# Dense layers in token order with expert results added onto them, and queries laid out like keys, in a fused attention and mixture-of-experts kernel

## The chip, the cores and the metric

The kernel runs on one core of a Trainium2 chip. The metric is the device time of one execution in microseconds (us). The five engines that matter are TensorE (PE, with its weight loads PEld), VectorE (DVE), ScalarE (ACT), GpSimd (POOL) and SyncE (SP). SP computes nothing: it issues most of the transfers, in the order of its own queue. POOL issues the indirect transfers (scatters) and the weight loads.

## The reference

Eight heads of sliding-window attention over 8 batches of 576 tokens are followed by a mixture of experts. Every token gets a dense two-layer result, and the result of the one expert with the largest gate logit, scaled by its probability:

```python
scores = scale * q @ k.T + bias; mask = (rel >= 0) & (rel < 128)
attn_out = softmax(where(mask, scores, -1e9)) @ v          # 8 x 8 x 576 x 64
x = attn_out.transpose(0, 2, 1, 3).reshape(4608, 512)
y_dense = relu(x @ w1_dense) @ w2_dense                     # 512 -> 512 -> 512
e = argmax(x @ w_gate); gate = softmax(x @ w_gate)[e]       # 8 experts
out = y_dense + gate * (relu(x @ w1[e]) @ w2[e])            # 4608 x 512, float32
```

## The kernel before

**Attention** runs in 16 units (`u`): a unit is one batch and four of its eight heads. A unit loads keys, queries and values (`load_k`, `load_q`, `load_v`, all on SP), turns keys and queries on DVE (`turn`, lines 310 and 313), rounds them on ACT (lines 319 and 323), makes scores on PE into the PSUM tiles `sq0` and `sq1` (lines 517 and 534), takes their exponentials on ACT (line 545, tile `p`), splits off a low part on DVE (line 555), multiplies with the values on PE (line 586, tile `ax`) and divides on DVE (`norm`, lines 604 to 616). `norm` of a batch's second unit ends with its last 64 rows, line 616. PE then transposes the result (line 646), and ACT copies it out of PSUM (line 655). Of the loads, `load_k` is one transfer with 4,608 bytes in a row; `load_q` is four transfers (one for each head) with 512 bytes in a row, because the queries come in another interleaving than the keys. The mask pattern and the list of token numbers (`place_f`) follow this interleaving.

**Routing**, once a batch: logits on PE, the choice of the expert and the position within it on DVE, and five scatters on POOL (`send`, line 809), which put the batch's rows of bfloat16, with gate and token number, into `xs_dram`, sorted by expert.

**Blocks.** A block is 128 rows of one expert, and there are 43 of them. Twenty are early: 11 may run after batch 4, another 9 after batch 6. The other 23 are late: they wait for all rows of the last batch. For a block, SP fetches the rows with a transposing transfer into `xTm` (line 958) and gate and token number into `xm` (line 961). DVE copies the expert's first weights (`bring`, line 997). PE runs `layer1` (line 1007) twice, once with the expert's weights and once with the dense ones; ACT applies relu twice; PE runs `layer2` (line 1019) twice; ACT scales the expert's result by the gate (line 1030); DVE adds the dense result (`sum_y`, line 1033); and POOL scatters the sum to the rows of the output (`store`, line 1037). So the dense layers run on the sorted rows too, 43 x 128 = 5,504 of them with the padding.

**Buffers** come from rings (`ROOMS`): `xm` has four places, which `store` still reads, early blocks have one `ye` and one `yo`, `stg` (turned keys and queries) has two. In the late blocks `p` (six places) holds weights and results.

**The order** on each engine is fixed before the run: a planner walks over the parts of the work, with costs, dependencies and wished times (`PACE`, `PLACE`, one offset and one step for each kind of part), and writes down an order for each engine. Engines and queues keep to it: an instruction that waits holds up all that stands behind it on its engine.

## Time and profile before

| | |
|---|---|
| runs of the kernel before | 420.17, 417.85, 414.70 us; median 417.85 |
| the profiled execution | 416.41 us, of which its trace spans 414.6 |
| mean granted clock of PE | 0.936 of full speed |
| busy: PE, DVE, POOL, ACT | 322.8, 269.4, 226.0, 203.3 us |
| DMA | 59.62 MB, mean 144 GB/s |

Busy time is the time in which an engine has an instruction under way. Matmuls are pipelined, so PE can count as busy while the next matmul is not yet needed. "Idle before" is an engine's pause in front of an instruction, with what ended it. The span divides into attention alone (to about 175 us), attention with early blocks (to about 283), routing of the last batch with the remaining early blocks (to about 319), and late blocks.

### The profile page before, as it was taken

The page shows a single profiled execution, that of the slowest core. Times are in us where ns is not written, and L with a number is a line of the kernel's source. Part 1 is how long each engine was busy: PE and PEld are TensorE (multiplying, and loading weights), DVE is VectorE, ACT ScalarE, POOL GpSimd, SP SyncE. Part 2 cuts the span into 40 slices and gives each one's busy share as a digit, 9 for nine tenths or more (in the row PEclk, how much of TensorE's full clock was granted, in tenths as well). Part 3 has the DMA queues.
Part 4 walks back from the last instruction along what each step waited for, and adds up shares of the span by engine and source line. Part 5 has one row for each costly group of instructions (what it writes and reads, how often), then busy time and mean ns, then how long its engine had stood idle before and what let it go on. Part 6 is the DMA issues. An engine that isn't in the chain of part 4 may idle for free.

```text
span 414.6 us, 12784 instructions
## 1 busy us (share of the span) xinstructions
PE 322.8 (78%) x5147; PEld 246.5 (59%) x5147; DVE 269.4 (65%) x454; ACT 203.3 (49%) x298; POOL 226.0 (55%) x269
## 2 busy tenths in 40 slices
PE   3326685876766766889798998997778879999993
PEld 0215574665665654777576776775556557767671
DVE  3268789799598898896778988755524322334331
ACT  4443564555544635474485675443243433544442
POOL 6065135996864858982668568485452422333332
PEclk9999689797769889699899999999999999999998
DMA  9994989889999967599897662125563332334430
GB/s 177 209 225 72 223 172 192 174 199 240 185 187 186 225 121 181 120 161 203 200 204 158 179 144 72 42 93 87 129 170 76 107 85 56 93 87 128 70 116 0
DMA packets 105961, 59.62 MB, mean 144 GB/s; under 512 B 71727, under 2 KB 100399, under 8 KB 105904
## 3 DMA queue, kind: packets, MB, share of 16 engines
q1 hardware_dynamic: 89952, 34.55, 42.3%
q0 software_dynamic: 14736, 23.68, 26.4%
q10 hardware_dynamic: 1216, 0.59, 0.8%
q8 instruction: 41, 0.67, 0.7%
q14 instruction: 16, 0.13, 0.1%
HBM read 47.29 MB, written 17.13 MB: 155 GB/s over the span
## 4 chain that ended last, share of the span: by engine, by line
PE 26%; DVE 25%; issue 21%; POOL 12%; DMA 10%; ACT 3%; SPq 2%; POOLq 1%; DVEq 0%; ACTq 0%
DVE p L555 11%; PE ax L586 10%; POOL out_dram L1037 8%; DMA out_dram<-yo,xm 5%; PE sq L534 4%; PE misc L1007 4%; DVE xf L605 3%; PE misc L1019 3%; DVE stg L310 3%; PE misc L646 3%; DMA vf<-in_v_dram 2%; DVE stg L313 2%; POOL xs_dram L809 2%; ACT p L545 1%; DMA rawq<-in_q_dram 1%
## 5 line engine op out<-in xcount | busy, mean ns | idle before, releaser
L555 DVE TENSOR_TENSOR p<-p 128x1024 bf16<-128x1024 f32 x64 | 101.2, 1609 | 10.6 <-ACT p L545 9.0
L586 PE MATMUL ax<-vf,p 128*128 128x65 bf16 (+3 forms) x1728 | 80.1, 208 | 11.1 <-DVE p L555 9.7
L586 PEld LDWEIGHTS <-p 128*128 128x128 bf16 (+1 forms) x1728 | 73.6, 110 | 19.7 <-DVE p L555 10.3
L545 ACT ACTIVATE p<-sq 128x1024 f32<-128x1024 f32 x64 | 63.2, 1022 | 31.9 <-PE sq L534 31.3
L809 POOL DMA_INDIRECT xs_dram<-xrow,slot x40 | 47.4, 1186 | 32.0 <-POOL xrow L806 9.3
L1037 POOL DMA_INDIRECT out_dram<-p,xm x23 | 24.7, 1076 | 55.0 <-DVE p L1033 55.0
L627 POOL CAST xrow<-xf 128x512 bf16<-128x512 f32 x32 | 35.7, 1117 | 32.8 <-DVE xf L605 32.7
L331 POOL TENSOR_TENSOR vf<-vf 128x1280 bf16<-128x1280 f32 x15 | 38.8, 2592 | 22.5 <-DMA vf<-in_v_dram 21.6
L1019 PE MATMUL misc<-w_all,hT 128*128 (+1 forms) x160 | 41.3, 384 | 7.8 <-DVE yo L1033 5.2
L1037 POOL DMA_INDIRECT out_dram<-yo,xm x20 | 24.7, 1236 | 33.3 <-DVE yo L1033 25.0
L1007 PEld LDWEIGHTS <-w_all 128*128 128x128 bf16 x688 | 40.2, 98 | 4.1 <-issue 2.9
L646 PE MATMUL misc<-ident_f,xf 128*128 128x128 f32 x128 | 24.3, 320 | 21.4 <-DVE xf L605 15.1
L1346 ACT ACTIVATE hT<-misc 128x512 bf16<-128x512 f32 x40 | 23.9, 598 | 34.3 <-PE misc L1007 34.2
L534 PE MATMUL sq<-qT,kT 32*128 32x256 f32 (+2 forms) x640 | 29.5, 314 | 10.9 <-ACT qT L319 10.0
L1277 ACT ACTIVATE xT<-sq 128x512 bf16<-128x512 f32 x46 | 25.0, 594 | 25.9 <-PE sq L1007 22.8
L655 ACT COPY xT<-misc 128x512 f32<-128x512 f32 x32 | 18.8, 587 | 34.0 <-PE misc L646 34.0
L534 PEld LDWEIGHTS sq<-qT,kT 32*128 32x128 f32 (+1 forms) x640 | 23.6, 206 | 18.5 <-ACT qT L319 11.4
L313 DVE STREAM_TRANSPOSE stg<-rawk 128x576 f32<-128x576 f32 x32 | 23.0, 759 | 14.2 <-DMA rawk<-in_k_dram 14.2
L1019 PEld LDWEIGHTS <-xT 128*128 128x128 bf16 x184 | 17.5, 98 | 23.9 <-ACT xT L1277 3.4
L646 PEld LDWEIGHTS misc<-ident_f,xf 128*128 128x128 f32 x128 | 15.9, 160 | 26.0 <-DVE xf L605 13.8
L1033 DVE TENSOR_TENSOR yo<-misc,ye 128x512 f32<-128x512 f32 x20 | 13.8, 688 | 23.7 <-DMA out_dram<-yo,xm 20.8
L517 PE MATMUL sq<-mask,ident 32*32 32x512 bf16 x512 | 20.4, 418 | 9.1 <-ACT p L545 7.2
(126 smaller groups left out, 531.7 us busy)
## 6 DMA issues: line engine op xcount, KB each, us to landing
rawk<-in_k_dram SPq DMA_DIRECT2D x16, 576.0 KB, 5.3
rawq<-in_q_dram SPq DMA_DIRECT2D x60, 144.0 KB, 5.3
vf<-in_v_dram SPq DMA_DIRECT2D x64, 128.0 KB, 4.8
w_all<-in_moe_w_dram POOLq DMA_DIRECT2D x16, 512.0 KB, 7.5
xs_dram<-fill_x SPq DMA_DIRECT2D x8, 130.0 KB, 2.0
w_all<-in_moe_w_dense_dram POOLq DMA_DIRECT2D x2, 512.0 KB
vf<-in_v_dram SPq DMA_DIRECT2D x16, 64.0 KB, 5.7
xTm<-xs_dram SPq DMA_TRANSPOSE x43, 4.1
```

Of the source, the lines that this page charges most:

```text
L313: nc.vector.transpose(out=s[:, c].rearrange("p (r x e) -> p r e x", r=R // 2, e=2), in_=raw[:, :, c].rearrange("p (r e) x -> p r e x", e=2),)
L331: eng.tensor_tensor(out=vb[:, :, :, 0:D, 0], in0=vf[:, :, :, 0:D], in1=vb[:, :, :, 0:D, 1], op=ALU.subtract,)
L534: nc.tensor.matmul(out=sq[g // 2][:nk, g % 2, PCOL[kj] : PCOL[kj] + nq], lhsT=kT[r0 : r0 + n, c, kj * P : kj * P + nk], rhs=qT[r0 : r0 + n ...
L545: nc.scalar.activation(out=p32, in_=T[(f"sq{p}", u, r)], func=ACT.Exp, scale=SCALE)
L555: nc.vector.tensor_tensor(out=lo, in0=T[("p", u, r, p)], in1=hi, op=ALU.subtract)
L586: nc.tensor.matmul(out=ax[:rows, i, o0 : o0 + w], lhsT=lhs, rhs=rhs, start=(n == 1), stop=(n == 3 * len(kl)),)
L627: nc.gpsimd.tensor_copy(out=xrows[b % 2].bitcast(BF16)[:, 2 * r : 2 * r + 2, hq * 256 : hq * 256 + 256], in_=T[("xf", u)][:, 2 * r : 2 * r ...
L646: nc.tensor.transpose(out=tp[:, i, c, :], in_=T[("xf", u)][:, 2 * r + i, c * P : c * P + P], identity=ident_f,)
L809: ins = nc.gpsimd.indirect_dma_start(out=xs_dram[:, :], out_offset=bass.IndirectOffsetOnAxis(ap=gst["slot", b][:rows, t : t + 1], axis=0), ...
L1007: nc.tensor.matmul(out=hp[:, c * P : c * P + P], lhsT=ws[:, kc, c * P : (c + 1) * P], rhs=xT[:, kc, :], start=(kc == 0), stop=(kc == 3),)
L1019: nc.tensor.matmul(out=y, lhsT=hT[:, c * P : c * P + P], rhs=w_all[:, E, 1, c, :] if dense else w_all[:, bass.DynSlice(er, 1), 1, c, :], s ...
L1037: ins = nc.gpsimd.indirect_dma_start(out=out[:, :], out_offset=bass.IndirectOffsetOnAxis(ap=T["xm", j][1].bitcast(I32)[:, 1:2], axis=0), i ...
```

## The change

The dense layers leave the blocks. Once a batch's attention is done, they run over its 576 rows in token order (`dense1`, `dense_relu`, `dense2`, `dense_out`), on a bfloat16 copy of the transposed result that ACT makes (`keep_b`, `keep_tail_b`), in the PSUM tiles `sq0`, `sq1` and `misc`; and SP stores them to the output (`dense_store`, three transfers a batch). A block then has the expert's layers alone, and its scatter adds onto the output in the transfer (`compute_op=ALU.add`). It waits for the dense stores of the batches that it can hold. `sum_y` is gone. Of the late blocks every second one (`ROWS`) is fetched as plain rows, into the space of the value buffers, and transposed on PE (`flip_rows`) with one more copy on ACT. Queries are loaded, turned and rounded as keys are: one transfer instead of four, two transposes on DVE instead of one. Rings change: `stg` 2 to 1, `hT` 3 to 2, `ye` 1 to 2, no `yo`, new `mt` (gate and token number, ten places) and `xr` (twelve). `PACE` and all of `PLACE` are new numbers.

```diff
-PACE = [11.15, 18.09]
+PACE = [10.39, 11.86]
...
-    "tt": (-36.78, 8.14), "vl": (-10.27, 9.4), "w": (24.71, 6.6), "xx": (2.02, 12.91),
+    "dy": (34.21, 3.45), "eb0": (-22.31, 9.54), "eb1": (31.4, 6.64), "ebt": (11.77, 12.23),
...
-        "stg": 2,
+        "stg": 1,
...
+        "mt": 10,
+        "xr": 12,
-        "hT": 3,
-        "ye": 1,
-        "yo": 1,
+        "hT": 2,
+        "ye": 2,
+        "xTb": 1,
+        "hTd": 1,
...
-    def load_q(u, h, eng):
...
-            out=t[32 * h : 32 * h + 32].rearrange("p (g r) c d -> p g (r c d)", r=2),
-            in_=q[b, 4 * hq + h].rearrange("(g p r) d -> p g (r d)", p=32, r=2),
+    def load_qk(u, nm, eng):
...
+            in_={"q": q, "k": k}[nm][b, 4 * hq : 4 * hq + 4].rearrange(
+                "h (p r) d -> (h p) (r d)", r=R
...
-        if nm == "q":
-            nc.vector.transpose(out=s.rearrange("p c (r x) -> p r c x", r=R), in_=raw)
-            return
         for c in range(2):
             nc.vector.transpose(
...
+    def keep_b(u, r):
...
+        nc.scalar.copy(
+            out=T[("xTb", b)][
+                :, 2 * hq : 2 * hq + 2, 2 * P * r : 2 * P * r + 2 * P
+            ].rearrange("p c (t x) -> p t c x", t=2),
+            in_=T[("misc", "tp", u, r)],
+        )
...
+    HS = S // 2
+
+    def dense1(b, c):
+        hp = buf((f"sq{c % 2}", "d", b, c), [P, 2, BANK], F32)
+        for i in range(2):
+            for kc in range(4):
+                nc.tensor.matmul(
+                    out=hp[:, i, 0:HS],
+                    lhsT=w_all[:, E, 0, kc, c * P : (c + 1) * P],
+                    rhs=T[("xTb", b)][:, kc, i * HS : (i + 1) * HS],
...
+    def dense_relu(b, c):
...
+        nc.scalar.activation(
+            out=T[("hTd", b)][:, c, :].rearrange("p (i x) -> p i x", i=2),
+            in_=T[(f"sq{c % 2}", "d", b, c)][:, :, 0:HS],
+            func=ACT.Relu,
...
+    def dense2(b, i):
+        tok = (f"sq{i}", "e", b, i) if i < 2 else ("misc", "e", b)
...
+        for t in range(2 if i < 2 else 1):
+            r0 = (2 * i + t) * P
+            rows = min(P, S - r0)
+            for c in range(4):
+                nc.tensor.matmul(
+                    out=y[:, t, :] if i < 2 else y[:rows, :],
+                    lhsT=T[("hTd", b)][:, c, r0 : r0 + rows],
+                    rhs=w_all[:, E, 1, c, :],
...
+    def dense_out(b, i):
+        t = buf(("p", "e", b, i), [P, 2, BANK], F32)
+        if i < 2:
+            nc.scalar.copy(out=t, in_=T["dy", b, i])
...
+    def dense_store(b, i):
...
+            ins = nc.sync.dma_start(
+                out=out[r0 : r0 + 2 * P, :].rearrange("(t p) d -> p t d", p=P), in_=t
+            )
...
+    ROWS = {j for j in range(NE, NB) if j % 2 >= OPT["rows"]}
...
+            moves = [(nc.sync.dma_start, xr.bitcast(I32), xs_dram[bass.DynSlice(r, P), :])]
...
+    def flip_rows(j, xp):
+        xr = T[("xr", j)].bitcast(BF16)
+        for c in range(4):
+            nc.tensor.transpose(
+                out=xp[:, c, :], in_=xr[:, c * P : c * P + P], identity=ident_b
+            )
...
-    def sum_y(j, yo, ye, y):
-        nc.vector.tensor_tensor(out=yo, in0=y, in1=ye, op=ALU.add)
...
             bounds_check=NTOK - 1,
             oob_is_err=False,
-        )
+            compute_op=ALU.add,
+        )
...
+            dense = [("ds", b, i) for b in range(nb) for i in range(3)]
...
-                "so", "POOL", 1.25, lambda j=j: store(j, T[("yo", j)]), after=[("yo", j)],
-                use=[("yo", j), ("xm", j)], move=0.6,
+                "so", "POOL", 1.25, lambda j=j: store(j, T["ye", j]), after=[("ye", j)] + dense,
+                use=[ot, meta], move=1.2, wait=True,
             )
```

## Rows read from the trace of the kernel before

**Rows 1.** The page: engines' busy time, and shares of the last-ending chain.

```profile
PE 322.8 (78%) x5147; PEld 246.5 (59%) x5147; DVE 269.4 (65%) x454; ACT 203.3 (49%) x298; POOL 226.0 (55%) x269
...
PE 26%; DVE 25%; issue 21%; POOL 12%; DMA 10%; ACT 3%; SPq 2%; POOLq 1%; DVEq 0%; ACTq 0%
```

**Rows 2.** Windows: stretch, length, busy PE, PEld, DVE, ACT, POOL, clock, DMA share, GB/s.

```profile
25.00:175.00 150.00, 106.16 (x2090) 87.76 (x2090) 129.96 (x209) 75.89 (x96) 100.86 (x89) 0.84 0.89 179
175.00:213.00 38.00, 32.66 (x593) 25.13 (x592) 29.20 (x47) 22.77 (x34) 21.29 (x18) 0.96 1.08 187
213.00:283.00 70.00, 65.08 (x1143) 50.17 (x1142) 56.79 (x103) 40.65 (x62) 49.70 (x58) 1.00 0.51 120
283.00:319.00 36.00, 27.60 (x324) 19.87 (x322) 15.11 (x41) 13.99 (x26) 16.78 (x26) 1.00 0.56 122
319.00:342.00 23.00, 18.64 (x203) 13.16 (x201) 7.29 (x11) 8.98 (x16) 7.36 (x12) 1.00 0.36 92
342.00:410.00 68.00, 65.13 (x728) 46.90 (x727) 23.69 (x35) 31.59 (x55) 23.18 (x37) 1.00 0.34 84
```

**Rows 3.** Timeline of PE, late blocks: start, us, engine, line, operation, count.

```profile
352.85 1.06 PE L1007 MATMUL sq<-xTm,p 128*128 128x128 bf16 x16
...
354.64 1.89 PE L1019 MATMUL misc<-w_all,xT 128*128 x8
...
359.88 1.06 PE L1007 MATMUL sq<-xTm,p 128*128 128x128 bf16 x16
...
405.55 1.89 PE L1019 MATMUL ax<-w_all,xT 128*128 x8
```

**Rows 4.** Timelines of DVE, POOL and PE around the end of attention.

```profile
282.45 0.41 DVE L616 TENSOR_TENSOR xft<-ax,recip 64x256 f32<-64x256 f32 x1
...
282.99 1.03 POOL L1037 DMA_INDIRECT out_dram<-yo,xm  x1 [0.19 <-DVE xft L616]
...
305.17 0.96 POOL L809 DMA_INDIRECT xs_dram<-xrow,slot  x1 [0.28 <-POOL xrow L806]
...
325.74 1.18 POOL L1037 DMA_INDIRECT out_dram<-yo,xm  x1 [3.31 <-DVE yo L1033]
...
319.27 1.06 PE L1007 MATMUL sq<-xTm,p 128*128 128x128 bf16 x16
```

**Rows 5.** Waits, DVE's and SP's queue: total us, times, longest.

```profile
DVE yo L1033 <- DMA out_dram<-yo,xm: 20.8, 9, 4.5
...
SPq L961 <- DMA out_dram<-yo,xm: 47.7, 15, 6.9
```

**Rows 6.** Timeline of DVE: two pauses for keys, at the start and in the middle.

```profile
23.92 1.44 DVE L313 STREAM_TRANSPOSE stg<-rawk 128x576 f32<-128x576 f32 x2 [9.33 <-DMA rawk<-in_k_dram]
...
198.90 1.44 DVE L313 STREAM_TRANSPOSE stg<-rawk 128x576 f32<-128x576 f32 x2 [4.03 <-DMA rawk<-in_k_dram]
```

**Rows 7.** Groups by line, DVE: busy us, mean ns of one, idle before.

```profile
L313 DVE STREAM_TRANSPOSE stg<-rawk 128x576 f32<-128x576 f32 x32 | 23.0, 759 | 14.2 <-DMA rawk<-in_k_dram 14.2
...
L310 DVE STREAM_TRANSPOSE stg<-rawq 128x1152 f32<-128x1152 f32 x16 | 21.8, 1364 | 4.6 <-DMA rawq<-in_q_dram 4.6
...
L1033 DVE TENSOR_TENSOR yo<-misc,ye 128x512 f32<-128x512 f32 x20 | 13.8, 688 | 23.7 <-DMA out_dram<-yo,xm 20.8 <-PE misc L1019 2.7
```

**Rows 8.** Groups by line, ACT's copies and exponentials out of PSUM.

```profile
L545 ACT ACTIVATE p<-sq 128x1024 f32<-128x1024 f32 x64 | 63.2, 1022 | 31.9 <-PE sq L534 31.3 <-PE ax L586 0.5
...
L655 ACT COPY xT<-misc 128x512 f32<-128x512 f32 x32 | 18.8, 587 | 34.0 <-PE misc L646 34.0
```

**Rows 9.** Transfers: issues, KB each where given, median us from issue to landing.

```profile
xTm<-xs_dram SPq DMA_TRANSPOSE x43, 4.1
...
xs_dram<-xrow,slot POOLq DMA_INDIRECT x40, 3.4
out_dram<-p,xm POOLq DMA_INDIRECT x23, 3.0
out_dram<-yo,xm POOLq DMA_INDIRECT x20, 4.4
```

More of the change, by code (lines that the diff above doesn't have):

```diff
@@ L20, with free @@
 FAR = 1.0e25
-LAG = {"PE": 0.3, "ACT": 0.2, "DVE": 0.2, "POOL": 0.2, "SP": 2.0, "PRE": 0.0}
-IN_TURN = "rawk rawq stg kT qT vf xf xft xT xTt xrow lt ax".split()
+LAG = {"PE": 0.3, "ACT": 0.2, "DVE": 0.2, "POOL": 0.2, "SP": 0.2, "PRE": 0.0}
+LANDING = 2.0
+IN_TURN = "rawk rawq stg kT qT vf xf xft xT xTt xTb hTd xrow lt ax xr".split()
 class Part:
+    def free(self):
+        return self.end + (LANDING if self.move else LAG[self.eng])
     __slots__ = "key eng cost fn kind at step want after take use move wait behind end".split()
@@ L130, in order @@
                     rooms[tok[0]].append(
-                        max(parts[k].end + LAG[parts[k].eng] for k in self.users[tok])
+                        max(parts[k].free() for k in self.users[tok])
                     )
@@ L342 @@
     )
-    load_k(0, nc.sync)
-    for h in range(4):
-        load_q(0, h, nc.scalar)
+    load_qk(0, "k", nc.sync)
+    load_qk(0, "q", nc.scalar)
     mask = consts.tile([P, H, 2 * PW], BF16, name="mask")
@@ L1045, in store @@
             oob_is_err=False,
+            compute_op=ALU.add,
         )
+        for x in range(nb, B):
+            tc.declare_no_dep(ins.ins, group=f"d{x}", reason="rows of later batches")
+        for x, name in dense_stores:
+            if x < nb:
+                tc.add_manual_dep(
+                    ins.ins,
+                    name,
+                    mybir.DependencyInfo(
+                        mybir.DependencyClass.Sync, mybir.DependencyReason.DATA
+                    ),
+                    reason="rows added to",
+                )
         tc.declare_no_dep(
@@ L1164 @@
             )
+            first = hq == 0 and r == 0
+            add(
+                ("eb", u, r), "ACT", 0.49, lambda u=u, r=r: keep_b(u, r), x, 0, f"eb{r}",
+                after=[("tp", u, r)], take=[("xTb", b)] if first else [],
+                use=[("misc", "tp", u, r)] + ([] if first else [("xTb", b)]),
+            )
         if hq < HQ - 1:
@@ L1255, in blocks @@
             one(
-                "fe", "SP", 2.3, lambda j=j: fetch(j), after=[("tc", s)] + rows,
-                take=[("xm", j)], move=0.75, wait=True,
+                "fe", "SP", 0.85 if j in ROWS else 2.2, lambda j=j: fetch(j),
+                after=[("tc", s)] + rows
+                + ([("pv", u, 1, p) for u in range(NU) for p in range(2)] if j in ROWS else []),
+                take=[("xr", j)] if j in ROWS else [("xm", j), ("mt", j)],
+                move=0.5 if j in ROWS else 0.75, wait=True,
             )
@@ L1325, in blocks @@
-                one(
-                    "ye", "ACT", 0.59, lambda j=j, f=ye: f(j), after=[("l2e", j)],
-                    use=[ot, yt[0], ("xm", j)],
-                )
-                one(
-                    "yo", "DVE", 0.61, lambda j=j, f=yo: f(j),
-                    after=[("l2d", j), ("ye", j)], use=[ot, yt[-1]],
-                )
-                one(
-                    "so", "POOL", 1.25, lambda j=j, ot=ot: store(j, T[ot][:, 1, :]),
-                    after=[("yo", j)], use=[ot, ("xm", j)], move=0.6,
-                )
@@ new lines, in blocks @@
+            one(
+                "l1e", "PE", 0.92, lambda j=j, f=l1: f(j),
+                after=[("xe" if j in ROWS else "fe", j)] + wts,
+                take=[ht] + ([] if j in ROWS else [htok]),
+                use=[("xm", j), wtok] + ([htok] if j in ROWS else []),
+            )
+            one("re", "ACT", 0.5, lambda j=j, f=re: f(j), after=[("l1e", j)], use=[htok, ht])
+            one(
+                "l2e", "PE", 0.95, lambda j=j, f=l2: f(j), after=[("re", j)],
+                take=[ytok, ot], use=[ht],
+            )
```

293 lines of the change are left out of this document (143 added, 150 removed), and 35 rows, old and new, of the table PLACE.

## The prediction

> **What bounds the kernel now.** I read the page first. PE is the busiest engine with 78% of the span, yet no engine holds more than about a quarter of the chain that ended last [rows 1]. So there is no single bound, and the stretches have to be read apart.
>
> The windows do that [rows 2]. From 25 to 175 us, attention runs alone. DVE is busy 130 of 150 us (87%). PE is busy 106, at a granted clock of 0.84, which is a mean over both levels. So DVE sets the pace, and PE has 44 us of gaps. From 175 to 283 early blocks run beside attention. From 213 to 283 PE is busy 65 of 70 us (93%) at full clock: there PE is the bound. From 283 to 342 (routing of the last batch, the remaining early blocks, the first late ones) PE falls back to 46 of 59 us with nobody full. From 342 to 410 PE is busy 65 of 68.
>
> What fills that last stretch is seen on PE's timeline [rows 3]: two blocks start 352.85 and 359.88, so one block costs 3.52 us. Two layer-1 groups of 16 matmuls take 354.64 - 352.85 = 1.79, so one takes 0.90. The four layer-2 groups of two blocks take the rest, 7.03 - 4 x 0.895 = 3.45, so 0.86 each. Expert and dense part each cost 1.76, and together they are the whole period: here PE is full.
>
> What holds 283 to 325 is not PE. Nine early stores start between 282.99 and 325.74 [rows 4], 5.3 us apart. DVE's sum waits for the store before it to land, because there is one `yo` (20.8 us in all) [rows 5]. The scatters of the last batch stand between these stores on POOL: attention ends with DVE's row at 282.86, the last scatter starts at 305.17, the first late matmul at 319.27, which is 36.4 us after the end of attention [rows 4]. SP waits 47.7 us for such stores before fetches, since `store` still reads `xm` [rows 5].
>
> **The change, part by part.** All sums are made against the profiled execution: 416.4 us, of which 1.8 lie outside the span of 414.6. It stands 0.3% under the median of the runs.
>
> *PE work.* The dense part of the blocks goes: 43 x 1.76 = 76 us. In its place, for each batch: layer 1 has 32 matmuls of 288 columns. By [rows 3] a column costs 0.895 us / 16 / 128 = 0.44 ns, so 32 x 0.126 = 4.0 us. Layer 2 has 20 matmuls of 512 columns, four of which cost 0.86, so 4.3. Together 8.3 us a batch, 67 in all. PE's work is nearly the same, therefore. The gain is in where it lies: four batches (33 us) can run before 175 us, in PE's gaps of 44 us. I cost that at nothing, because DVE sets the pace there and the dense layers use no DVE. Without that cover it costs up to 33 us.
>
> *ACT work.* For each batch four copies of 512 columns (0.59 each) and a small one (taken as 0.4), four relus of 576 (between 0.59 and 1.02, nearer the first: 0.65), and two copies of 1,024 (1.02) with a short one (0.6) [rows 8]: 2.4 + 0.4 + 2.6 + 2.6 = 8.0 us. Up to 175 us that adds 32 to 76 busy of 150 [rows 2], hidden there. The blocks lose one relu each, about 0.6 x 43 = 26.
>
> *DVE work.* The sums go: 0.69 each [rows 7]; about eleven lie before 283 us, so 7.6. Turning queries takes two transposes of 0.76 in place of one of 1.36 [rows 7], 0.15 more a unit. Over the ten units up to 175 us, where DVE is the bound, that costs 1.5 us. With one `stg`, the second transpose waits for ACT to round the first. DVE has low parts to do meanwhile, so I take nothing; the upper bound is 1.2 us a unit, about ACT's copy of 1,024 columns [rows 8], 12 us in ten units.
>
> *Loads on SP.* One issue replaces four per unit. DVE waited 9.33 us for the keys of unit 1, and 4.03 us for keys near 199 [rows 6]. The first pause comes from the order: queries were wished ahead of keys (`ldq` -22.8, `ldk` 27.7), and their load waits until unit 0's queries are turned. Now keys come first (-14.54, -13.22). Everything on DVE stood behind that pause, so its end is worth at most 9.33. I take 6, since the low parts of unit 0 were already due and only their start moves. The lower bound is 0.
>
> *Middle, 175 to 283.* PE loses 11 x 1.76 = 19.4 and gains two batches, 16.7. DVE loses 7.6 and the 4.03 pause may go. I take -6, with bounds of -16 (PE no longer the limit) and +10 (the dense layers wait for `sq0` and `sq1`, and scores queue behind them). The end of attention then lies at 282.9 - 6 + 1.5 - 6 = 272.4.
>
> *Routing and early stores.* Two `ye` and no sum break the 5.3 us rhythm. Five scatters with little between them, after routing, need about 8 + 8 us, their landing 3.4, the fetch 4.1 [rows 9]. So the first late matmul comes about 24 us after attention in place of 36.4 (bounds 20 and 36).
>
> *Late blocks.* PE needs 1.76 and, for every second block, four transposes (a quarter of a layer-1 group, 0.22): 1.87 a block. The other engines have had, per block of 3.52 (68 / 3.52 = 19.3 blocks), ACT 1.63, DVE 1.23, POOL 1.20, and lose work or keep it [rows 2]. The scatter that adds isn't in the trace. The transfer engines were busy 0.34 x 68 / 19.3 = 1.2 us a block for fetch and store; that is the lower bound. Twice that, 2.4, is the upper one, if each row is read as well as written. I take a period of 2.2, between PE's need and this.
>
> The Trainium skill ("DMA: Bandwidth & Descriptors", Rules for kernel authors) speaks against the added scatter: an accumulating transfer reads its destination and writes it later, so it moves more than the plain one. By that rule the period would be up to 2.4 and the time 4 us later; by the row of plain stores it would be PE's 1.87 and 7 us earlier. No row here shows an add.
>
> *Sum of the tail.* After attention PE still has nine early blocks (16), the last batch's dense layers (8.3), routing (taken as 5) and 23 late blocks (43): 72 us, at the 93% of [rows 2] 77.6. The other way, 24 + 22 x 2.2 + 3.5 for the last block's own chain = 75.9. The larger counts. Before, the last layer 2 ended at 407.4 [rows 3], 7.2 before the end. The add lands later than a plain store (3.0 or 4.4 [rows 9]); I add 1.5 of a possible 0 to 4: 8.7. In sum 272.4 + 77.6 + 8.7 + 1.8 = 360.5, so **361 us**.
>
> **The rivals.**
> *A: DMA becomes the bound of the first stretch.* For: its share is 0.89 at 179 GB/s there, and 1.08 right after [rows 2]; four batches of dense stores add 4.7 MB, at the full rate of 179 / 0.89 = 201 GB/s 23 us. Against: 16 us of share are free, and DVE rarely waits for loads. Between +7 and +23: about 376 us.
> *B: the dense layers get into the path of attention.* They take `sq0` and `sq1` six times a batch, and scores wait for these. With all of the 33 us before 175 us exposed, 394. For: one order for each queue. Against: PE's 44 us.
> *C: better than that.* The early blocks are done when attention ends, and the late ones run at 1.95. Attention ends at 262, then 24 + 43 + 3.5 + 8.7 + 1.8: 343 us. Against: DVE's 87% leave little.
> *D: the dense layers don't run in the gaps.* `dy` is wished 34 us after its unit, three units late. If two more batches fall behind attention, PE has 17 us more there and less before: about 371.
> *E: slower, by the adds alone.* Every late block goes through one scatter. To lose the whole gain of 55 us, 23 blocks need 2.4 us more each, so 4.6 us an add, and for 2% slower 5.0. At 5.5 us the time is 437. For: a store of before takes 3.0 to 4.4 to land, and reads could come on top one after another. Against: these are latencies, which overlap; a store's own share is at most 1.2.
>
> **How the numbers follow.** Forecast 0.52 (by itself 348 to 374), A 0.14, B 0.11, C 0.11, D 0.05, E 0.06, no change 0.01. About 2% is what a measurement of this kernel can tell from no change. Below 2% faster lie all but E, the worst of B, and no change: faster 0.90, within 2% 0.04, slower 0.06. The range runs from C to B, 343 to 392; E, no change and the ends of B and C are left out.
>
> **What the profile of after would show.** Right: dense matmuls spread from about 60 us on, PE's share in the first 175 us near 90%, a higher granted clock there, units 15 us apart as before; no pause of 9 us for unit 1's keys; early stores closer than 4 us; late blocks about 2.2 us apart. Wrong: units further apart with DVE waiting for exponentials (B) or loads (A); dense matmuls bunched after attention (D); late stores over 3 us apart with PE waiting and adds landing late (E).

## The result, and the profile after

The changed kernel takes 385.2 us (median of four runs, 381.6 to 388.3), against 417.4 for the kernel before (414.7 to 420.2): a ratio of 0.920, with a 95% interval of 0.910 to 0.930. The forecast was 361, with a range of 343 to 392. The direction and the range held; of the 55 us that were expected, 32 came. 385 lies outside the forecast's own band (348 to 374), between the rivals A and B. The profiled execution took 388.3 us, 386.6 of them its span, and everything below is read from that one unless another kernel is named. Some executions of every kernel here, this one among them, run in a slower state and take some per cent longer, so the times of the experiments are those of their fast runs, while marks inside an execution come from its profiled one, which is slow in dense_quarter (379.3 us), weights_apart (391.6), late_in_turn (386.3) and queries_kept_stage1 (419.2).

The page first: busy time of each engine, and the shares of the chain that ended last.

```profile
PE 312.1 (81%) x4719; PEld 228.6 (59%) x4747; DVE 242.1 (63%) x426; ACT 242.8 (63%) x362; POOL 251.1 (65%) x265
...
PE 38%; DVE 17%; DMA 15%; POOL 12%; issue 7%; ACT 7%; SPq 1%; POOLq 0%; ACTq 0%; DVEq 0%
```

Against [rows 1], DVE has fallen from 25% to 17% of the chain and PE has risen from 26% to 38%. The windows, with the columns of [rows 2], show where:

```profile
25.00:175.00 150.00, 126.61 (x2138) 94.86 (x2142) 118.46 (x189) 97.64 (x139) 94.02 (x86) 0.92 0.83 197
...
283.00:319.00 36.00, 30.45 (x306) 20.86 (x309) 12.69 (x39) 19.91 (x35) 25.96 (x33) 0.97 0.94 171
319.00:342.00 23.00, 18.36 (x161) 12.19 (x164) 4.95 (x7) 11.05 (x20) 12.83 (x16) 0.82 1.04 139
342.00:380.00 38.00, 29.07 (x321) 21.11 (x324) 8.38 (x12) 22.48 (x38) 29.69 (x32) 1.00 0.93 121
```

From 25 to 175 us PE is busy 127 where it was 106, as meant. But DVE, which had set the pace with 130, is busy only 118: it now waits for something. At the other end, PE is busy only 29 of the 38 us from 342 on, where it was full before.

Three marks on DVE and PE divide the time. These are timelines: the last row of attention on DVE, the first late matmul (line 1083 is an expert's layer 1) and the last layer 2 on PE.

```profile
282.55 0.42 DVE L598 TENSOR_TENSOR xft<-ax,recip 64x256 f32<-64x256 f32 x1
```

```profile
316.49 1.49 PE L1083 MATMUL sq<-xm,p 128*128 128x128 bf16 x16
...
377.31 1.02 PE L1095 MATMUL ax<-w_all,xT 128*128 x4
```

Attention ends at 282.97, where it ended before (282.86) [rows 4]. The first late matmul comes at 316.49 in place of 319.27: 2.8 us gained. From there to the end of the last layer 2 it takes 61.8 us (378.3 - 316.5) in place of 88.1 (407.4 - 319.3) [rows 3, 4]: 26.3 gained. From there to the end, 8.3 in place of 7.2: 1.1 lost. Sum 28.0, the difference of the spans (414.6 - 386.6). So nearly the whole gain is the dense work that left the late blocks. The early part, which took that work in, came out even, though loads and sums had been taken from it. That is where the forecast's missing 27.8 us begin:

| | forecast, us | measured, us | difference |
|---|---|---|---|
| end of attention | 272.4 | 283.0 | +10.6 |
| to the first late matmul | 24 | 33.5 | +9.5 |
| to the end of the last layer 2 | 53.6 | 61.8 | +8.2 |
| to the end of the span | 8.7 | 8.3 | -0.4 |

The new wait is DVE's. From the list of waits (who waited for whom: total us, times, longest):

```profile
DVE recip L586 <- PE ax L568: 34.2, 19, 7.3
...
ACT p L527 <- DMA out_dram<-p: 8.5, 7, 2.4
...
DVE stg L310 <- ACT kT L317: 4.8, 3, 3.4
```

The first of these, DVE's reciprocals waiting for the attention's products, was 7.0 us before:

```profile
DVE recip L604 <- PE ax L586: 7.0, 9, 2.6
```

One place where the dense layers stand in the way, on PE, ACT and DVE (start, us, engine, line, operation, count, and in brackets the idle time before):

```profile
65.08 5.39 PE L679 MATMUL sq<-xTb,w_all 128*128 128x288 bf16 x32
70.30 1.46 PE L568 MATMUL ax<-vf,p 128*128 128x65 bf16 x36
```

```profile
67.21 0.65 ACT L690 ACTIVATE hTd<-sq 128x576 bf16<-128x576 f32 x1 [4.79 <-PE sq L679]
...
70.07 1.24 ACT L317 CAST kT<-stg 128x1152 fp32r<-128x1152 f32 x1
```

```profile
71.34 1.44 DVE L310 STREAM_TRANSPOSE stg<-rawq 128x576 f32<-128x576 f32 x2 [3.41 <-ACT kT L317]
```

All 32 matmuls of a batch's dense layer 1 run in one piece, and the attention's product (line 568) stands behind them. ACT stands 4.79 us waiting for its relus, with the rounding of the keys queued behind them. DVE stands 3.41 us because the only staging buffer is free only after that rounding. Such waits for the staging buffer sum to 4.8 us here and to 1.4 in another execution of the same kernel (after_again). In this place the wait falls on a turn. In front of a reciprocal it stands where attention ends, on PE and DVE:

```profile
274.75 3.61 PE L704 MATMUL sq<-w_all,hTd 128*128 128x512 bf16 x15
...
278.63 2.83 PE L568 MATMUL ax<-vf,p 128*128 128x65 bf16 x72
```

```profile
281.50 0.21 DVE L586 RECIPROCAL recip<-ax 128x8 f32<-128x8 f32 x1 [3.74 <-PE ax L568]
```

A piece of dense layer 2 (line 704) runs ahead of the last products of attention, and DVE waits 3.74 us for these.

### The profile page after: what moved, and what is told of

Read it like the earlier page. It is cut to its first block, busy times and chain, and to the rows that moved or that the text cites. A ratio compares the mean times of both kernels' runs of the same rounds, so it can differ in the third digit from the quotient of the medians.

```text
span 386.6 us, 11917 instructions
## 1 busy us (share of the span) xinstructions
PE 312.1 (81%) x4719; PEld 228.6 (59%) x4747; DVE 242.1 (63%) x426; ACT 242.8 (63%) x362; POOL 251.1 (65%) x265
## 3 DMA queue, kind: packets, MB, share of 16 engines
HBM read 48.73 MB, written 26.57 MB: 195 GB/s over the span
## 4 chain that ended last, share of the span: by engine, by line
PE 38%; DVE 17%; DMA 15%; POOL 12%; issue 7%; ACT 7%; SPq 1%; POOLq 0%; ACTq 0%; DVEq 0%
PE ax L568 11%; POOL out_dram L1112 10%; DMA out_dram<-p 8%; DVE p L537 7%; PE sq L679 5%; PE sq L704 4%; DVE stg L310 4%; PE sq L516 3%; PE misc L1095 3%; ACT p L527 3%; PE misc L628 3%; PE misc L1083 2%; DMA vf<-xs_dram 2%; PE sq L499 2%; DVE xf L587 2%
## 5 line engine op out<-in xcount | busy, mean ns | idle before, releaser
L325 POOL TENSOR_TENSOR vf<-vf 128x1280 bf16<-128x1280 f32 x15 | 37.2, 2482 | 15.9 <-DMA vf<-in_v_dram 15.8
L1112 POOL DMA_INDIRECT out_dram<-ye,mt x20 | 37.9, 1897 | 14.2 <-ACT ye L1106 10.8
L1073 DVE COPY p<-w_all 128x2048 bf16 x23 | 16.1, 724 | 45.4 <-DMA out_dram<-p,vf 27.1
L679 PE MATMUL sq<-xTb,w_all 128*128 128x288 bf16 x256 | 35.6, 293 | 1.6 <-ACT p L527 1.4
L704 PE MATMUL sq<-w_all,hTd 128*128 128x512 bf16 x120 | 30.3, 394 | 3.3 <-ACT p L527 2.7
L679 PEld LDWEIGHTS <-w_all 128*128 128x128 bf16 x256 | 24.6, 100 | 9.2 <-issue 2.2
L690 ACT ACTIVATE hTd<-sq 128x576 bf16<-128x576 f32 x32 | 20.7, 652 | 14.9 <-PE sq L679 14.7
L1111 POOL MEMSET junk<- 128x1 f32 x43 | 29.9, 696 | 0.0
L1073 DVE COPY ws<-w_all 128x2048 bf16 x20 | 16.1, 803 | 21.6 <-PE misc L1083 21.5
L317 ACT CAST qT<-stg 128x1152 fp32r<-128x1152 f32 x16 | 19.8, 1240 | 12.7 <-DVE stg L310 7.3
L586 DVE RECIPROCAL recip<-ax 128x8 f32<-128x8 f32 x32 | 6.4, 199 | 34.2 <-PE ax L568 34.2
```

The source lines that it names most:

```text
L325: eng.tensor_tensor(out=vb[:, :, :, 0:D, 0], in0=vf[:, :, :, 0:D], in1=vb[:, :, :, 0:D, 1], op=ALU.subtract,)
L679: nc.tensor.matmul(out=hp[:, i, 0:HS], lhsT=w_all[:, E, 0, kc, c * P : (c + 1) * P], rhs=T[("xTb", b)][:, kc, i * HS : (i + 1) * HS], star ...
L704: nc.tensor.matmul(out=y[:, t, :] if i < 2 else y[:rows, :], lhsT=T[("hTd", b)][:, c, r0 : r0 + rows], rhs=w_all[:, E, 1, c, :], start=(c ...
L1112: ins = nc.gpsimd.indirect_dma_start(out=out[:, :], out_offset=bass.IndirectOffsetOnAxis(ap=T["mt", j].bitcast(I32)[:, 1:2], axis=0), in_= ...
```

## The experiments

Twelve kernels were run, in four groups; each group shared runs of the kernel before on its chip. The changed kernel itself, unaltered, stood in the first.

**after_again.** No edit.

> The changed kernel unaltered, beside the three experiments, so that their traces have one of the same chip to stand against. Expected 382 to 387 us, the end of attention (last 64-row product on VectorE) at 279 to 284 us of the span, 2.4 us from one late store to the next.

It took 390.5 us on that chip, where the kernel before took 416.9. Attention ended at 284.8, the late adds were 2.39 us apart (22 intervals from 329.8 to 382.5), and DVE waited 32.4 us for the attention's products. The next three are read against it.

**dense_quarter.** A quarter of the dense products.

```diff
-            for kc in range(4):
+            for kc in range(1):
...
-            for c in range(4):
+            for c in range(1):
```

> Of each dense matmul group one of four is left (one chunk of 128 of the contraction in either layer), so the dense result is incomplete; the order on every engine, the relus, the copies and the dense stores are as in the changed kernel. Theory P (dense matmuls stand in front of attention's on TensorE and hold up exponentials and divisions): TensorE's dense busy time falls from 74 to about 19 us, VectorE's waits for the attention products fall from 34 us to under 15, attention ends at 268 to 275 in place of 283, and the time is 370 to 377. Theory D (the transfers that came with the change are what slows attention): attention ends within 3 us of the unaltered kernel, and the time is within 4 us of it.

Ratio to before 0.895 (0.864 to 0.926), 373 us: some 17 us under after_again. The last row of attention, on DVE:

```profile
276.45 0.42 DVE L598 TENSOR_TENSOR xft<-ax,recip 64x256 f32<-64x256 f32 x1
```

Attention ends at 276.9, 7.9 us earlier than in after_again, with the same transfers, copies, relus and stores. DVE's wait for the attention's products falls from 32.4 to 23.9. So the dense matmuls are not free: three quarters of them cost 8 us by the end of attention, and 6.5 of the 8 are there when unit 10's queries are turned (164.5 against 170.9). Theory P is right in kind and was too large: 26.5 us of dense work are left in place of 19, the waits are not under 15, and attention ends 2 us past its 275. The granted clock from 25 to 175 us is lower as well (0.89 against 0.93 in after_again), so the attention's own matmuls do not run alike in the two.

What is left of the waits is not all the dense layers' doing. The longest of them, 7.31 us in the changed kernel (it ends at 147.11), is here too, with 6.81 us: transposes stand ahead of the product in PE's order, and they wait for a division on DVE. That is the new order, and no run takes it apart. And 276.9 is still not 272.4; something else holds it as well.

**plain_scatter.** The scatter of expert rows writes and does not add, so the outputs lack the dense part.

```diff
-            compute_op=ALU.add,
```

> The block results overwrite the rows of the output instead of being added, so the dense result is lost there; nothing else differs. Theory D (adds load the transfer engines): a store lands in 3 to 4 us in place of 5 to 6, GpSimd's instruction takes 1.0 in place of 1.57 us, the transfer engines' share in the late blocks falls from 0.93 to about 0.55, the period falls from 2.4 to 2.0 us, and the time is 367 to 375. Theory C (the late period is TensorE's and ScalarE's own chain): landing falls, but the period stays above 2.25, and the time is 379 to 384.

Ratio 0.921 (0.906 to 0.937), 383 us, 8 under after_again. Its late stretch in the windows:

```profile
342.00:370.00 28.00, 22.90 (x244) 16.07 (x244) 6.24 (x9) 17.30 (x29) 12.87 (x24) 1.00 0.43 129
```

The late stores are 2.35 us apart (22 intervals from 320.5 to 372.1). The share of the transfer engines has fallen to 0.43, which is 1.0 us a block (0.43 x 28 / 11.9 blocks), where the adds take 2.2 (0.93 x 38 / 15.9). Half the engines' time, and the same period: the adds do not set it. The Trainium skill's rule that the prediction weighed ("DMA: Bandwidth & Descriptors", Rules for kernel authors: an accumulating transfer reads its destination) agrees with this doubling of the share. The read itself is not seen: the pages count the same bytes with the add and without it (48.73 MB read, 26.57 written). The period that the prediction derived from the rule is refuted. What the adds cost lies elsewhere: a start on GpSimd mostly takes 1.57 us in place of 0.98, and the gain appears before the late blocks (attention ended at 280.2 in place of 284.8, first late store 320.5 in place of 329.8). Why attention gains from it was not traced.

**weights_apart.** The late blocks' copied weights in the keys' buffers, free by then, and not in the ring that also holds the results under way to the output.

```diff
-            wtok = ("p", "w", j) if late else ("ws", j)
+            wtok = ("kT", "w", j) if late else ("ws", j)
```

> Late blocks' weights take the two places of the turned keys, which are free by then, so that the six places of p hold late results alone. Theory R (the period of late blocks is set by the ring: a place is held until its add has landed, and VectorE's next weights wait for it): VectorE's waits for landings (42 us) vanish, the period falls from 2.4 to 2.0 us, and the time is 372 to 378. Theory D (the transfer engines are full by then, 0.93): the period stays at 2.3 to 2.4 us, other waits take the place, and the time is within 4 us of the unaltered kernel.

Ratio 0.920 (0.888 to 0.952). DVE no longer waits for a landing; in the waits from 335 to 380 us stands in its place

```profile
DVE kT L1073 <- PE sq L1083: 30.6, 9, 3.8
```

and the adds are 2.37 us apart (331.4 to 383.5). So DVE's 27 us of waits for landings, the largest late wait in the changed kernel's list, was a wait beside the path. What is left is PE itself. Its timeline over one pair of late blocks in the changed kernel (line 1095 is layer 2, 1051 the four transposes of a block that was fetched by rows):

```profile
345.85 1.02 PE L1095 MATMUL misc<-w_all,xT 128*128 x4 [0.16 <-issue]
346.71 1.95 PE L1083 MATMUL sq<-xm,p 128*128 128x128 bf16 x32
350.28 1.02 PE L1095 MATMUL ax<-w_all,xT 128*128 x4 [1.62 <-ACT xT L1401]
351.14 0.39 PE L1051 MATMUL sq<-ident,vf 128*128 128x128 bf16 x4
351.58 0.81 PE L1095 MATMUL misc<-w_all,xT 128*128 x3
```

Both layer 1 of a pair run together (x32). Then PE has nothing but the two layer 2, whose inputs ACT is just making, and it waits, here 1.62 us. Before, two dense layer 1 stood in that place [rows 3] and hid the relus.

**late_in_turn.** TensorE's order of the late blocks made to alternate, by two added conditions.

```diff
-                after=[("xe" if j in ROWS else "fe", j)] + wts,
+                after=[("xe" if j in ROWS else "fe", j)] + wts
+                + ([("l2e", j - 2)] if late and j - 2 >= NE else []),
...
-                after=[("re", j)],
+                after=[("re", j)] + ([("l1e", j + 1)] if late and j + 1 < NB else []),
```

> The changed kernel with one thing altered: in the late blocks TensorE's order is made to alternate (layer 1 of a block, layer 2 of the block before it, layer 1, layer 2), where the changed kernel runs the two layer 2 of a pair, then both layer 1, and then waits some 0.95 us for ACT's relu. Theory C (the late period of 2.40 us is the chain PE, ACT, PE of a pair with nothing on PE to hide the relu): that wait goes, the period falls to 1.9 to 2.1 us, the 22 late blocks take 7 to 10 us less, total 7 to 10 us below the unaltered changed kernel (378 where that is 386). Theory T (the accumulating transfers, 2.2 us of the DMA engines per block, set the period): 2.2 to 2.4 and a total within 4 us of 386. Attention ends where it does in the changed kernel (283 to 285) by both.

Ratio 0.915 (0.905 to 0.925), 380.5 us. PE's timeline:

```profile
361.04 1.06 PE L1083 MATMUL sq<-xm,p 128*128 128x128 bf16 x16
361.93 1.03 PE L1095 MATMUL misc<-w_all,xT 128*128 x4
362.79 1.06 PE L1083 MATMUL sq<-xm,p 128*128 128x128 bf16 x16
363.69 1.03 PE L1095 MATMUL ax<-w_all,xT 128*128 x4
364.60 0.38 PE L1051 MATMUL sq<-ident,vf 128*128 128x128 bf16 x4
364.82 1.06 PE L1083 MATMUL sq<-xm,p 128*128 128x128 bf16 x16
```

A pair takes 3.78 us (364.82 - 361.04), without a gap. Over all 22 intervals the adds are 2.18 us apart (330.2 to 378.2), and 2.02 over the last 15; one interval of 5.65 us (342.3 to 348.0) lies in the rest. Theory C holds for the cause: the period was PE waiting for ACT, by the order. Over the whole stretch its 1.9 to 2.1 us is not reached. The late blocks take 48.0 us in place of 52.6. In the total this is 0.6% against the changed kernel's ratio of 0.920 and 2.3% against after_again (390.5 of 416.9), which the intervals do not tell apart from nothing. Here GpSimd comes into sight as the next limit: two adds in a row start 1.87 us apart.

```profile
357.96 1.57 POOL L1112 DMA_INDIRECT out_dram<-p,mt  x1 [0.19 <-ACT xm L1424]
...
359.83 1.57 POOL L1112 DMA_INDIRECT out_dram<-p,vf  x1 [0.19 <-issue]
```

**sends_ahead.** As late_in_turn, and no early add from block 13 on before the last batch's five sends.

```diff
-                after=[("ye", j)] + dense,
+                after=[("ye", j)] + dense + ([("sx", B - 1, NT - 1)] if j > 12 else []),
```

> As late_in_turn, and on GpSimd the five sends of the last batch's rows go ahead of the two early scatter-adds that stand among them in the changed kernel's order (all the early adds from block 13 on come after the last send). Theory Q (the late blocks' start waits for the last send, and each add ahead of it costs its 1.6 us of GpSimd): last send and first late matmul 3 to 4 us earlier (313 in place of 316.5), total 3 to 4 us under late_in_turn. Rival Q0: the early blocks still hold PE and the p buffers until 324, or the adds that are pushed behind (3.9 us apart) delay the late ones: no gain or a loss of up to 5 us.

Ratio 0.920 (0.908 to 0.932), 382.8 us: no gain over late_in_turn. GpSimd's timeline, the last send and the last early add:

```profile
305.42 0.95 POOL L868 DMA_INDIRECT xs_dram<-xrow,slot  x1 [0.28 <-POOL xrow L865]
...
327.29 1.55 POOL L1112 DMA_INDIRECT out_dram<-ye,mt  x1 [1.27 <-DMA mt<-xs_dram]
```

The last send ends 22.2 us after attention (306.4 - 284.2) in place of 25.5 in the changed kernel, 3.3 earlier as theory Q has it. But the first late matmul stands at 319.5, where late_in_turn has it at 319.9: the early adds were only pushed behind, and the last one starts at 327.3. Rival Q0 is right.

**small_stores.** The dense stores cut to a small part; most of the output is left unwritten by them.

```diff
-            ins = nc.sync.dma_start(
-                out=out[r0 : r0 + 2 * P, :].rearrange("(t p) d -> p t d", p=P), in_=t
-            )
+            ins = nc.sync.dma_start(out=out[r0 : r0 + P, 0:128], in_=t[:, 0, 0:128])
```

> The changed kernel with nearly all of the dense layers' store left out: each store of 256 rows writes 128 rows by 128 columns only (the last 64 rows of a batch are stored whole), so 8.1 MB of writes go and everything else stays, the adds and what waits for a store among it. Theory P (the first stretch is held by dense products standing ahead of the attention's on TensorE): attention ends within 2 us of the changed kernel's 283 to 285, total within 4 us of 386; what may go is the 8.5 us that ACT's exponentials waited in all for a p buffer whose store had not landed, of which at most a few us lie on the path. Theory D (the dense stores crowd the transfers of keys, queries and rows): attention ends 5 us or more earlier, the keys' and queries' landing falls from 8.9 towards 5.3 us, total 375 or less.

382.4 us, where the kernel before took 416.6 on that chip. Attention ends at 281.6:

```profile
281.18 0.42 DVE L598 TENSOR_TENSOR xft<-ax,recip 64x256 f32<-64x256 f32 x1
```

DVE's wait for the attention's products stays at 30.6. ACT's waits for a `p` buffer whose store had not landed fall from 8.5 us (5.4 in after_again) to 1.3. So the stores, 7.3 MB less of them by the pages, are worth 1 to 3 us of attention (281.6 against 283.0 and 284.8), and they do not hold the first stretch (the prediction's rival A).

**queries_only.** On the kernel before: queries loaded, turned and rounded as keys are, tokens in natural order, and nothing else of the change. The core of it:

```diff
-    def load_q(u, h, eng):
+    def load_qk(u, nm, eng):
...
-            out=t[32 * h : 32 * h + 32].rearrange("p (g r) c d -> p g (r c d)", r=2),
-            in_=q[b, 4 * hq + h].rearrange("(g p r) d -> p g (r d)", p=32, r=2),
+            in_={"q": q, "k": k}[nm][b, 4 * hq : 4 * hq + 4].rearrange(
+                "h (p r) d -> (h p) (r d)", r=R
+            ),
```

> The kernel before with one part of the change alone: queries loaded by one transfer a unit, turned in two instructions and rounded with the permuting copy, as the keys are, tokens in natural order; no dense part is moved, the staging ring stays at 2. By the forecast's steps: the loads of unit 1 are no longer behind eight small query loads, so the pause of 9.33 us at 23.92 shrinks by about 6, the turns cost 0.15 us more a unit, total 4 to 6 us under the kernel before (412 where that is 417). Rival N (what follows is bound by VectorE's own order and not by the loads): the pause only moves, first low parts at 25 to 26 in place of 26.5, total within 2 us of the kernel before.

Neither: ratio 1.029 (1.020 to 1.038), slower. The first stretch gains what was foreseen. In the kernel before, the queries of units 0 and 1 were turned here, on DVE:

```profile
11.55 1.38 DVE L310 STREAM_TRANSPOSE stg<-rawq 128x1152 f32<-128x1152 f32 x1 [4.55 <-DMA rawq<-in_q_dram]
...
25.28 1.33 DVE L310 STREAM_TRANSPOSE stg<-rawq 128x1152 f32<-128x1152 f32 x1
```

Now those of unit 1 are turned at 21.42, and unit 9's attention is done 8 us sooner (last rows at 165.8 in place of 173.9). But attention ends at 282.8 again, the last early add starts at 334.9 in place of 325.7, and the late stretch takes 89.8 us in place of 81.1. The planner had made the order anew with wishes that fitted the old parts. PE's timeline in the late blocks (984 layer 1, 996 layer 2) shows one of its effects:

```profile
378.02 1.06 PE L984 MATMUL sq<-xTm,p 128*128 128x128 bf16 x16
...
382.48 1.89 PE L996 MATMUL ax<-w_all,xT 128*128 x8 [0.65 <-ACT xT L1253]
...
385.93 1.06 PE L984 MATMUL sq<-xTm,p 128*128 128x128 bf16 x16
```

All four layer 1 of a pair run first, then the layer 2 wait for a relu: 7.9 us for a pair that took 7.03 [rows 3]. To see the part without the order, the next two keep the old order by hand.

**queries_kept_order.** The same edit, with the planner given the old parts and costs, so that every engine's order is that of the kernel before.

```diff
-                    lambda u=u, h=h: load_q(u, h, nc.sync), u, h,
+                    lambda u=u, h=h: None if h else load_qk(u, "q", nc.sync), u, h,
```

> The edit of queries_only (one load a unit, two turns, permuting copy, natural token order) on the kernel before, but with the instruction order of the kernel before held fixed: the planner is given the old parts and costs, and three of its four query loads issue nothing. Theory O (queries_only lost by its newly made order, above all by late blocks at 3.2 us in place of 2.35): late adds again 2.35 us apart, unit-1 queries turned at 21.4 to 22 in place of 25.28, and the total 4 to 8 us under the kernel before (409 to 413 where that is 417). Rival B (from 213 us on TensorE is 93% busy, and what the loads give is swallowed there): unit 9's attention 4 to 8 us ahead, attention ends at 281 to 283 all the same, total within 2 us of the kernel before.

Ratio 0.985 (0.978 to 0.993), 410.6 us against 416.1: 5.5 us gained. DVE's timeline at the start:

```profile
20.04 1.44 DVE L304 STREAM_TRANSPOSE stg<-rawk 128x576 f32<-128x576 f32 x2 [6.30 <-DMA rawk<-in_k_dram]
21.40 1.40 DVE L304 STREAM_TRANSPOSE stg<-rawq 128x576 f32<-128x576 f32 x2
```

Attention ends at 279.4, 3.5 us earlier, the last early add is 4.8 earlier, the end 5.2. Theory O holds for the start and the total. Its 2.35 us between late adds is a misreading: they come 2.37 and 4.65 us apart in turn, here as in the kernel before. Most of the gain at the start is there with the first unit: its queries are turned at 8.06 in place of 11.55, without the wait of 4.55 us for their load.

**queries_kept_stage1.** The same, with one staging buffer.

```diff
-        "stg": 2,
+        "stg": 1,
...
-    plan = Plan(ROOMS)
+    plan = Plan(dict(ROOMS, stg=2))
```

> queries_kept_order with one staging buffer for turned keys and queries in place of two, again with the same instruction order. The forecast's step (one buffer costs nothing, bound 12 us): within 2 us of queries_kept_order. Rival S (VectorE's second turn of a unit has to wait until ACT has rounded the first, and ACT stands in the exponentials): queries of unit 1 turned at 23.5 to 25, some 0.3 to 3 us of VectorE waiting per unit on the kT copy, first stretch 3 to 12 us longer, total 3 to 10 us above queries_kept_order.

Ratio 0.999 (0.994 to 1.004), 416.5 us. The 5.5 us are gone. DVE's timeline at the start:

```profile
20.48 1.44 DVE L304 STREAM_TRANSPOSE stg<-rawk 128x576 f32<-128x576 f32 x2 [6.32 <-DMA rawk<-in_k_dram]
23.17 1.44 DVE L304 STREAM_TRANSPOSE stg<-rawq 128x576 f32<-128x576 f32 x2 [1.26 <-ACT kT L311]
```

Between the two turns of a unit DVE now waits until ACT has rounded the keys: 7.7 us in five such waits. The rest is not in that line. In the profiled executions, 419.2 and 411.5 us long, attention ends 7.8 us later than with two buffers (287.2). Rival S holds.

**quarter_stage2.** dense_quarter with two staging buffers, order unchanged; the room comes from keeping a quarter of the dense hidden layer, so outputs lack what dense_quarter lacks and more.

```diff
-        "stg": 1,
+        "stg": 2,
...
-            buf(("hTd", b), [P, 4, S], BF16)
+            buf(("hTd", b), [P, 1, S], BF16)
```

> dense_quarter (a quarter of the dense layers' products, everything else of the changed kernel there) with two staging buffers for turned keys and queries in place of one, all engines' orders as in the changed kernel; the room for it comes from keeping a quarter of the dense hidden layer. Theory S2 (the single staging buffer costs the changed order some 6 us as it cost the order before): VectorE's waits for ACT's kT copy go, attention ends 4 to 7 us earlier than dense_quarter's 276.9, at 270 to 273, which is where the forecast had put it, total 4 to 7 us under dense_quarter's 371 to 375. Rival S0 (with the dense products in front of the attention the staging was covered): attention ends at 276 to 278, total within 2 us of dense_quarter.

DVE's last row of attention:

```profile
269.97 0.42 DVE L598 TENSOR_TENSOR xft<-ax,recip 64x256 f32<-64x256 f32 x1
```

Attention ends at 270.4, 6.5 us before dense_quarter's and 2 before the forecast's 272.4: for the attention S2 holds. The 6.5 compare executions of 375.3 and 379.3 us on two chips, so a part of them may be no more than that difference. The lead is 3.7 us at unit 2's queries (35.15 against 38.81), 2.2 at unit 10's (162.3 against 164.5), and the rest comes behind. DVE's waits for ACT's `kT` copy, 2.9 us in dense_quarter, are gone. For the total S2 does not hold: 372.8 us, with the kernel before at 412.4 on that chip (0.90), as dense_quarter (0.895). In its profile, the last early add starts 43.5 us after attention (313.9), in dense_quarter 39.3 (316.2). So two thirds of the gain were given back between attention and the late blocks.

**three_early_buffers.** As sends_ahead, with three result buffers for early blocks, the room taken from their gates.

```diff
-        "mt": 10,
+        "mt": 6,
-        "ye": 2,
+        "ye": 3,
...
-    plan = Plan(ROOMS)
+    plan = Plan(dict(ROOMS, ye=2, mt=10))
```

> The sends_ahead kernel with three buffers in place of two for the results of the early expert blocks (and six in place of ten small ones for their gates), all engines' orders as in sends_ahead. Theory Y (after the attention each early add is let go by the landing of the add two before it, 6.4 us, so they come 3.5 us apart and hold GpSimd until 327): the early adds after the attention come 2.2 to 2.8 us apart, the last of them at 312 to 318, the late adds start 8 to 12 us earlier at 1.9 to 2.1 us each, total 371 to 375. Rival PE (TensorE, 85% busy from 283 to 319, sets the pace of the early blocks): 3.2 to 3.5 us apart as before, total 379 to 383.

Ratio 0.924 (0.914 to 0.934), 385.9 us: no gain over sends_ahead (0.920). The four early adds before the sends stay 3.4 us apart, so there two buffers were not the limit. The four after the sends come 1.9 to 2.4 apart, as theory Y has it, and then GpSimd stands still for 8 us, because PE does:

```profile
320.19 0.61 PE L1051 MATMUL sq<-ident,vf 128*128 128x128 bf16 x4 [5.39 <-DMA vf<-xs_dram]
```

In PE's order a late block's transposes stand ahead of the last early blocks, and its rows arrive at 320, some 13 us after the last send (306.25 + 0.95). Whether the shorter ring of gates delays that fetch was not tried.

## Why the prediction was right or wrong

The direction is right, and what kept the time inside the range is the room left for rivals: of the four parts of the sum, three came out 8 to 11 us longer than forecast. Of its signs, the dense matmuls from 65 us on, the higher clock (0.92 against 0.84) and early stores closer than 4 us (3.4) are there. So is the one for rival B, units further apart (16.5 us in place of 15.3 between the queries of units 3 and 10), though DVE waits for products and not for exponentials.

**The dense layers, near in size, wrong in price.** PE's dense groups are 35.6 + 30.3 + 8.3 = 74 us, 9.3 a batch (forecast 8.3); 8 matmuls are missing from this trace, and after_again, with all of them, has 76. ACT's parts came out as priced: 600 ns for a copy of 512 columns, 652 for a relu, 1,030 and 575 for the copies out. The step that failed is "I cost that at nothing, because DVE sets the pace there". PE did have 44 us of gaps, but a gap is a place in a queue's order, and the dense matmuls stood in whole blocks of 4 to 5 us ahead of products that DVE waited for. This is rival B, by the order of the queue. Its other reason, scores that wait for `sq0` and `sq1`, shows little: PE's waits for ACT to free them grew from 7.2 to 9.8 us. dense_quarter measures 8 us at the end of attention for three quarters of the dense matmuls, which is a quarter of the 33 that B had.

**One staging buffer, "I take nothing".** This failed as well: 6.5 us at the end of attention in one pair of executions (quarter_stage2), and 6 us of the total in the old order (queries_kept_stage1), which is the firmer of the two. The bound of 12 held. The forecast argued that DVE has low parts to do meanwhile. In a fixed order it does not do them: it waits at its next instruction.

**The loads, right in size, in part by another cause.** The 6 us of the prologue are there when the staging buffer doesn't take them. In quarter_stage2 unit 2's queries are turned at 35.15, where the kernel before did it at 41.08. The forecast put the gain down to the order, in which queries were loaded ahead of keys. But queries_kept_order keeps that order and has 4.0 of the 6 (37.06), 3.5 of them at unit 0's queries. Their load in four transfers had held DVE for 4.55 us, a wait that stands in [rows 7] (4.6) and that the forecast did not price. In the changed kernel unit 2's queries are turned at 39.48. Unit 1's keys land in time there,

```profile
17.50 1.44 DVE L310 STREAM_TRANSPOSE stg<-rawk 128x576 f32<-128x576 f32 x2 [6.31 <-DMA rawk<-in_k_dram]
...
23.88 1.44 DVE L310 STREAM_TRANSPOSE stg<-rawq 128x576 f32<-128x576 f32 x2
```

but the order puts a preparation of `vf` and all constants between the two turns, so little of the 6 us shows at once.

**The middle, right in size.** From 171 to 283 us the changed kernel makes up 7 us (unit 10's queries turned at 171.3 in place of 164.5, attention's end the same). The forecast had 6. Its reason, PE as the bound of this stretch, is not borne out: with three quarters of the dense matmuls gone the stretch is only 1.4 us shorter (112.4 in dense_quarter, 113.9 in after_again). So luck may have a part in it.

That puts the miss of 10.6 us ahead of the middle. By the forecast's terms unit 10's queries would be turned at 160.0 (164.5 - 6 + 1.5), 11.4 us earlier than they were. There dense_quarter gains 6.5 and the second staging buffer 2.2 more. So the two prices of nothing make up about 8.7 of the 11.4. The rest is open: a quarter of the dense matmuls is left in both runs, and ACT's 8 us a batch, which the forecast took as hidden, were not taken out by themselves.

**Routing, 24 against 33.5, failed in two terms.** The timeline of GpSimd after attention:

```profile
294.42 1.83 POOL L1112 DMA_INDIRECT out_dram<-ye,mt  x1 [1.16 <-DVE ni L882]
296.32 0.22 POOL L865 TENSOR_SCALAR xrow<-tok_c 128x1 int32<-128x1 f32 x1
...
298.19 1.58 POOL L1112 DMA_INDIRECT out_dram<-ye,mt  x1 [0.19 <-ACT hTd L690]
...
307.51 0.95 POOL L868 DMA_INDIRECT xs_dram<-xrow,slot  x1 [0.28 <-POOL xrow L865]
```

Until the first send it takes 13.4 us (296.3 - 283.0), not 8. The kernel before already needed 12.6 until its first send of the last batch started (295.5), so no row stood behind the 8. The sends take 12.1 (to 308.5), not 8, for two adds stand among them. Landing and fetch take 8.0, as foreseen (7.5). sends_ahead won the two adds back and gained nothing in all, since the early adds behind them then hold the late blocks. This stretch has several limits close together, and the runs moved one or two of them. What sets the 13.4 was not taken apart.

**The late period, 2.2 against 2.39, near in size, wrong in cause.** The forecast chose between PE's 1.87 and a doubled transfer share of 2.4. The share did double, as plain_scatter shows, and did not matter. The period was PE's 1.87 and a wait for the relu that the dense part had hidden. late_in_turn reaches 2.02 at its best with the same adds. Nor was it the lower clock at the start of that stretch (0.82 from 319 to 342 us): from 342 us on, at full clock, the adds are 2.38 apart as well. The forecast priced what the removed dense layers cost and not what they covered. The sum "72 us at 93%" for the tail became 77.9 us at 80% (30.45 + 18.36 + 29.07 of 97). The forecast's prices for the add, 4 us later or 7 us earlier, also slip: they count 22 periods, but the larger of two tails was taken, so a period of 2.4 makes the time 2.7 us later (80.3 for 77.6) and one of 1.87 changes nothing.

**The end, right:** 8.3 against 8.7, with the adds landing in 5.2 to 6.4 us (3.0 and 4.4 before [rows 9]).

Of the kernels that compute the whole output, late_in_turn has the lowest ratio: 0.915 of the kernel before. That it beats the changed kernel is seen in its late period and not settled by the totals.

## What to carry to other kernels

Idle time of an engine is cover only for work that its order puts into that idle time: before pricing moved work at nothing, find what stands behind each block of it in the same queue, and who waits for that. When work is removed from a loop, ask what latency it hid, and turn the order of the loop around so that something else hides it. When an order is made anew, try a part of the change under the old order too: queries_only lost 3% with the same edit that gained 1.5% in the old order.

## What the runs showed of the hardware

A scatter that adds costs the issuing engine more too: mostly 1.57 us of GpSimd for 128 rows of 2 KB, where the plain one in the same kernel (plain_scatter) took 0.98. It lands later, 5.2 to 6.4 us after its issue in place of 3.0 to 4.4 in the kernel before [rows 9], though the other transfers beside it were not the same:

```profile
out_dram<-ye,mt POOLq DMA_INDIRECT x20, 6.4
out_dram<-p,mt POOLq DMA_INDIRECT x12, 5.8
out_dram<-p,vf POOLq DMA_INDIRECT x11, 5.2
```

A share of the transfer engines of 0.93 in the late window was no proof that they set the pace: with 0.43 the late period was the same. The granted clock of the first stretch, a mean over the two levels of 1.2 and 2.4 GHz, was 0.84 with 106 us busy before [rows 2], 0.89 with 109 in dense_quarter, 0.92 with 127 in the changed kernel, and 0.85 with 115 in quarter_stage2. It was higher where TensorE was busy most, but not strictly, and no run was made on it.
